# Four pairs' scores in other PSUM banks, products of ones on TensorE in the planned gaps of the first batches, and keys and values pooled by VectorE in one instruction each

## The chip, the cores and the metric

The kernel runs on one NeuronCore of a Trainium2 chip. The metric is the device time of one execution in microseconds (us), lower is better. The core has five engines, each with an instruction queue of its own that is worked off in order: PE (TensorE, matrix products; PEld is its loading of the stationary operand), DVE (VectorE), ACT (ScalarE), POOL (GpSimd) and SP (SyncE, which only issues transfers here). PE writes only to PSUM, which here holds eight tiles ("banks") of 128x512 fp32. Engines wait for each other through semaphores.

## The reference, cut to what matters

Three stages follow one another on 8 batches of 576 rows, 8 heads of 64, model width 512:

```python
def _attn_ref(q, k, v):                       # q, k, v: (8, 8, 576, 64)
    k_p = k.reshape(B, H, 72, 8, D).mean(axis=3)
    v_p = v.reshape(B, H, 72, 8, D).mean(axis=3)
    scores = scale * np.matmul(q, k_p.transpose(0, 1, 3, 2))
    attn = softmax(scores)                    # written out in the original
    return np.matmul(attn, v_p)

def _moe_ref(x, U, V, w_ch1, w_ch2):          # x: (8, 576, 512)
    h = x.transpose(0, 2, 1) @ U @ V
    u = x + h.transpose(0, 2, 1)
    return u + np.maximum(u @ w_ch1, 0.0) @ w_ch2

def _moe2_ref(x, g_ln, w_ch1, w_ch2):         # layer norm, then a second MLP
    xn = (x - mu) / np.sqrt(var + 1e-06) * g_ln
    return x + np.maximum(xn @ w_ch1, 0.0) @ w_ch2
```

Keys and values are averaged over groups of 8 rows ("pooled") before the attention uses them.

## The kernel before

**Two stages.** The first stage (phase_a) takes the attention of one batch after the other, the low-rank step with U and V, and, one group of 512 rows behind it, a first half of the first MLP (8 of its 16 blocks of hidden units, weights resident in SBUF). The second stage (passes) streams the rest of the first MLP and the second MLP through the banks; the change leaves its code alone.

**A pair of heads.** The attention works on 32 pairs of heads, four for each batch. For pair P: load keys, queries and values (att_load); pool the keys and scale them into kbd (att_prep); pool the values into vs (att_prep_v); five products for the scores, 3 of them into one bank and 2 into another (att_s, line 847); a minimum over each row by DVE and ten exponentials by ACT (att_m); ten transposes by PE of the result, copied to SBUF as ef (att_t, transposes at line 398). In the first two batches (P < TM = 8) values follow with the sums of the softmax in an extra column (tm_v, line 1029), DVE divides (tm_n, tiles sm, xg, x), and PE multiplies by U (tm_g, line 1086). At the end of a batch come transposes of xg (tm_t), a copy and a subtraction that make gs (att_gs), products with V (tm_u, line 1120) and the split of the result into two fp32r parts, hid, which is the operand of the MLP (ACT and DVE). The MLP's two layers in the first stage are a_l1 (line 1291, banks "pa", two of them) and a_l2 (line 1319, banks "pbc", two). The other four banks, "py", serve all of the attention. For batch one, tm_g and tm_t also use the MLP's banks, which are idle then.

**Pooling before.** Keys: one TENSOR_REDUCE over 576 elements on DVE, or three adds on POOL, whichever the planner finds sooner done. Values: three adds that halve 512 columns per head to 256, 128 and 64 (lines 818 to 831), each one on DVE or POOL.

**Who sets the order.** A planner (Order.schedule) runs at build time. Every operation has a list of engines with a planned cost, a priority that comes from its place in the program and a bias, and the tiles it uses; the planner steps through planned time and gives each engine its next ready operation. What comes out is a fixed order of instructions for every engine; the chip then works through it in its own time, and only semaphores keep it right. PE's planned cost is doubled while the planner takes TensorE for cold (warm, SLOW).

**Resident weights.** load_w decodes 16 half blocks of 64-bit weights on DVE (four instructions of 128x512, lines 601 to 621), ACT rounds the upper part (wh), and the lower part (wl) is a subtraction, on POOL alone before the change (line 556).

Of the kernel before, what the change touches and what calls it, by code (L numbers as in the profile page):

```python
# [14 lines left out]
ALU = mybir.AluOpType  # L15
AX = mybir.AxisListType
# [6 lines left out]
POOL = 8  # L23
# [78 lines left out]

class Order:
    def __init__(self, nc, tc):
        self.nc, self.tc, self.ops, self.clk, self.bias = nc, tc, [], 0.0, 0.0

    def op(self, engs, fn, r=(), w=(), prio=None, size=0, full=False):
        o = Op()
# [42 lines left out]
    def schedule(self):  # L151
# [61 lines left out]
        while left:  # L213
# [50 lines left out]
                got = other_mode[2]  # L264
            for x in later:
                heapq.heappush(av, x)
            if got is None:
                if later:
                    at(e, t + 150)
                if fut:  # L270
                    at(e, fut[0][0])
                continue
# [93 lines left out]
def c_dve(n):  # L366
    return 68 + 1.042 * n
# [10 lines left out]
def c_pool(n):  # L378
    return 147 + 2.11 * n
# [42 lines left out]
class Kern:  # L422
    def __init__(self, nc, tc, aps):
        self.nc, self.tc = nc, tc
        (self.qT, self.kT, self.v, self.U, self.V, self.wA, self.g, self.wC, self.out) = aps
        self.w_raw = [self.wA, self.wC]
        self.o = Order(nc, tc)
        att = Pool("att")
        stg = Pool("stg")
        slots = Pool("slots", side="right")  # L430
        w = Pool("wres", side="right")
        b1 = Pool("b1", after=[att])
        b2 = Pool("b2", side="right", after=[w])
        ps = Pool("ps", space=PSUM)
        self.pools = [stg, att, slots, w, ps, b1, b2]
        R = self.R = {}

        def ring(pool, name, shape, dt=F32, n=1, fifo=True):
            R[name] = Ring(pool, shape, dt, n, name, fifo)

        ring(stg, "wraw", [128, 512], I64)
        ring(stg, "wx", [128, 512])
        ring(stg, "wt", [128, 512])
        ring(att, "araw", [128, 512], I64)
        ring(att, "ax", [128, 512])
        ring(att, "at", [128, 512])
        ring(att, "kbd", [128, 2, SP], n=2)
        ring(att, "q", [128, S], n=2)
        ring(att, "k", [128, S])
        ring(att, "v", [SP, 2, POOL * D])  # L450
        ring(att, "kp", [128, SP], n=2)
        ring(att, "vs", [SP, 4, D], F32R, 3)
        ring(att, "vz", [SP, 3 * D], n=2)
        ring(att, "ef", [SP, 2, S])
        ring(att, "sc", [128, 5, 2 * SP], n=2)
        ring(att, "mx", [128, 10], n=2)
        ring(att, "sm", [128, 10], n=2)
        ring(att, "eh", [SP, 2, S], F32R)
        ring(att, "el", [SP, 2, S], F32R)
        ring(att, "avt", [128, SH], n=2)  # L460
        ring(att, "xT", [128, S], n=5)
        ring(att, "xh", [128, DM], F32R, 2)
        ring(att, "xl", [128, DM], F32R, 2)
        ring(att, "gr", [128, DM], F32R)
        ring(att, "gs", [128, DM], F32R)
        ring(att, "ust", [128, 5, 128], F32R)
        ring(att, "us", [128, 5, 128])
        ring(att, "vd", [128, S // 4], F32R, 2)
        ring(att, "v1", [SP, 2, D + 1], n=2)
        ring(att, "x4", [128, DM])  # L470
        ring(att, "ut", [128, 4 * 64])
        ring(att, "vstk", [128, S], F32R)
        ring(slots, "op", [128, SLOT], F32R, 16)
        ring(slots, "hid", [128, SLOT], F32R, 8)
        for f in range(NA):
            for a in "hl":
                ring(w, f"w{a}{f}", [128, 1024], F32R)
        ring(w, "xg", [128, NCC, TG])
        ring(w, "ys", [128, TG], n=2)
        for j in range(NSL):  # L480
            pool = b1 if j < NSL - 1 else b2
            for a in "hl":
                ring(pool, f"w1{a}{j}", [128, 7, 256], F32R)
                ring(pool, f"w2{a}{j}", [128, 2, 512], F32R)
        ring(b1, "xraw", [128, NCC, TG])
        ring(b1, "t3", [128, 2, TH])
        ring(b1, "t2", [128, 2, TH])
        ring(b2, "s12", [128, TG], n=2)
        ring(b2, "s5", [128, TH], n=2)
        ring(b2, "res", [128, NCC, TG], n=2)  # L490
        ring(b2, "yt", [128, NCC, TG])
        for a in ("lnh", "lnl"):
            ring(b2, a, [128, TG], F32R)
        for a in ("lns", "lnq"):
            ring(b2, a, [128, TG])
        for a in ("lnv", "lnd"):
            ring(b2, a, [128, TG // 128])
        ring(ps, "pa", [128, 512], n=2)
        ring(ps, "pbc", [128, 512], n=2, fifo=False)
        ring(ps, "py", [128, 512], n=4)  # L500
# [244 lines left out]
    def load_w(self, f, z, way):  # L745

        if z == 0:
            self.wres[f] = self.buf(f"wh{f}"), self.buf(f"wl{f}")
        wh, wl = self.wres[f]
        x = self.decoded(0, f, z, way)  # L750
        c = slice(z * 512, z * 512 + 512)
        self.split(View(wh, z, lambda t: t[:, c]), View(wl, z, lambda t: t[:, c]), View(x, None, lambda t: t), 512, hi_on=(ACT,), lo_on=(GP,))

    def ahead(self, layer, f, z):

# [32 lines left out]
    def att_prep(self, P):  # L788
# [2 lines left out]
        kp, kbd = self.buf("kp"), self.buf("kbd")  # L791
        kv = lambda: k.t.rearrange("p (n s) -> p n s", s=POOL)

        def pool(e):
            if e is nc.vector:
                e.tensor_reduce(kp.t, kv(), axis=AX.X, op=ALU.add)
                return
            for n in (4, 2):
                e.tensor_add(kv()[:, :, :n], kv()[:, :, :n], kv()[:, :, n : 2 * n])
            e.tensor_add(kp.t, kv()[:, :, 0], kv()[:, :, 1])  # L800

        o.op({DVE: c_dve(S), GP: c_pool(4 * SP) + c_pool(2 * SP) + c_pool(SP)}, pool, w=[k, kp])
        for h in range(2):
            r = slice(64 * h, 64 * h + 64)
            o.op(
# [7 lines left out]
    def att_prep_v(self, P):  # L813
# [1 line left out]
        v = self.raw[P][2]  # L815
        vs = self.vs[P] = self.buf("v1" if P < TM else "vz" if P < LEAN_T else "vs")
        n = POOL * D
        while n > D:
            n //= 2
            to, w = (lambda n=n: v.t[:, :, :n]), [v]  # L820
            if P < LEAN_T and n == D:
                to, w = (lambda: vs.t.rearrange("p (a d) -> p a d", d=D)[:, 0:3:2]), [v, vs]
                if P < TM:
                    to = lambda: vs.t[:, :, :D]
            o.op(
                {GP: c_pool(2 * n), DVE: c_dve(2 * n)},
                lambda e, n=n, to=to: e.tensor_add(to(), v.t[:, :, :n], v.t[:, :, n : 2 * n]),
                w=w,
            )
        if P < LEAN_T:  # L830
            return
        self.split(
            View(vs, 0, lambda t: t[:, 0:4:3]),
            View(vs, 1, lambda t: t[:, 1:3]),
            View(v, None, lambda t: t[:, :, :D]),
            2 * D,
        )

    def att_s(self, P, t):
        q, kbd = self.qk[P]  # L840
        if t in (0, 3):
            self.sps[P, t // 3] = self.buf("py")
        ps = self.sps[P, t // 3]
        i = t % 3 * 2 * SP
        self.o.op(
# [498 lines left out]
    def phase_a(self):  # L1344
# [2 lines left out]
        self.xT, self.xhl, self.ut, self.hid, self.wres = {}, {}, {}, {}, {}  # L1347
        self.ud, self.yd, self.wd = {}, {}, {}
        per = self.att_steps()
        self.lean = False  # L1350
        for st in self.biased(per[0], E_BIAS):
            st()
# [476 lines left out]
LAST = ((0, 0), (0, 1), (1, 0), (0, 2), (1, 1), (0, 3), (1, 2), (1, 3))  # L1829
P_BIAS = -20000.0  # L1830
BACC = {"dynamic_dma_scratch_size": 2048}
TM = 2 * NP
E_BIAS = -40000.0
LEAN_T = 8
LEAN_X = 8
W_LEAD = (-12000.0, 8000.0)
# [50 lines left out]
```

## Time and profile before

| what | value |
|---|---|
| runs shown | 1757.46, 1762.2, 1763.09 us, median 1762.2 |
| profiled execution | 1756.11 us, its span 1754.3 us |
| PE busy | 1729.4 us, 99% of the span |
| DVE, ACT, POOL busy | 959.6, 714.5, 753.9 us |

The span runs from the first to the last instruction; the time of the execution has 1.8 us more around it. Busy shares are averages over stages that differ: PE is nearly always busy after the first 100 us, and DVE is busiest in that first part.

### The profile page before, as it was taken

What the parts mean: (1) busy time and instruction counts of PE and PEld (TensorE: products, weight loads), DVE (VectorE), ACT (ScalarE), POOL (GpSimd) and SP (SyncE); (2) the same over time, 40 slices, a digit from 0 to 9 for tenths busy, and PEclk for the clock granted to TensorE, in tenths of its full rate; (3) what the DMA queues carried; (4) which work ended last, traced back from release to release, by engine and by line L of the source; (5) the groups of instructions that cost most, each with busy time, mean ns of one, the idle gap of its engine ahead of it and who ended that gap; (6) DMA issues with size and microseconds to landing.
All of it is one profiled execution on the core that took longest, in us unless ns stands there. A gap on an engine that the chain in (4) does not pass through costs nothing.

```text
span 1754.3 us, 27128 instructions
## 1 busy us (share of the span) xinstructions
PE 1729.4 (99%) x10302; PEld 1525.7 (87%) x10302; DVE 959.6 (55%) x1839; ACT 714.5 (41%) x1812; POOL 753.9 (43%) x655
## 2 busy tenths in 40 slices
PE   6999999999999999999999999999999999999998
PEld 6888888888888899999999889999999999999997
DVE  7998887888655344444445756553225633333333
ACT  5765655655522233333333443333333332223221
POOL 3442312311100166666667643333335455555554
PEclk9999999999999999999999999999999999999999
DMA  6665554555143334444443453431112422333322
GB/s 201 217 201 170 184 182 147 179 174 162 55 165 108 130 111 121 121 121 121 120 121 115 126 163 125 134 121 67 49 49 85 144 103 103 110 119 103 103 79 78
DMA packets 96691, 222.99 MB, mean 127 GB/s; under 512 B 15408, under 2 KB 15792, under 8 KB 90800
## 3 DMA queue, kind: packets, MB, share of 16 engines
q1 hardware_dynamic: 96416, 221.26, 39.9%
q8 instruction: 80, 1.31, 0.3%
q14 instruction: 51, 0.42, 0.1%
q10 hardware_dynamic: 144, 0.00, 0.0%
HBM read 151.85 MB, written 69.37 MB: 126 GB/s over the span
## 4 chain that ended last, share of the span: by engine, by line
PE 91%; DVE 2%; DMA 1%; POOL 0%; issue 0%; ACT 0%; DVEq 0%; POOLq 0%; ACTq 0%
PE py L1608 33%; PE pa L1520 17%; PE pbc L1520 13%; PE pbc L1319 11%; PE pa L1291 11%; PE py L398 2%; PE py L847 2%; PE py L978 1%; PE py L979 1%; PE py L1016 0%; PE py L1015 0%; DVE w1l L556 0%; PE py L1185 0%; PE pbc L1743 0%; DMA wraw<-w_d 0%
## 5 line engine op out<-in xcount | busy, mean ns | idle before, releaser
L1608 PE MATMUL py<-hid,w2h 128*128 128x512 f32 x1728 | 541.2, 394 | 0.2 <-DVE hid L1548 0.2
L1608 PE MATMUL py<-hid,w2l 128*128 128x512 f32 x864 | 338.7, 392 | 0.0
L1520 PE MATMUL pa<-op,w1h 128*128 128x256 f32 x1728 | 326.2, 281 | 1.4 <-DVE s L405 1.0
L1520 PEld LDWEIGHTS pa<-op,w1h 128*128 128x128 f32 x1728 | 293.8, 188 | 37.9 <-DVE s L405 1.5
L556 POOL TENSOR_TENSOR op<-xraw,op 128x512 fp32r<-128x512 f32 x130 | 171.9, 1324 | 276.9 <-ACT op L403 272.0
L1578 DVE TENSOR_TENSOR pbc<-s,pbc 128x512 f32<-128x512 f32 x108 | 75.2, 696 | 382.2 <-PE pbc L1520 382.2
L1608 PEld LDWEIGHTS py<-hid,w2h 128*128 128x128 f32 x1728 | 273.7, 189 | 11.1 <-DVE hid L1548 0.5
L1520 PEld LDWEIGHTS pbc<-op,w1h 128*128 128x128 f32 x1296 | 220.8, 188 | 28.1
L1520 PE MATMUL pbc<-op,w1h 128*128 128x256 f32 x1296 | 244.3, 281 | 0.0
L1520 PE MATMUL pa<-op,w1l 128*128 128x256 f32 x864 | 242.7, 281 | 0.0
L1608 PEld LDWEIGHTS py<-hid,w2l 128*128 128x128 f32 x864 | 162.5, 188 | 36.7
L1319 PE MATMUL pbc<-op,wh 128*128 128x512 f32 x576 | 182.1, 397 | 0.0
L1520 PE MATMUL pbc<-op,w1l 128*128 128x256 f32 x648 | 181.8, 281 | 0.0
L1291 PE MATMUL pa<-hid,wh 128*128 128x512 f32 x576 | 180.5, 394 | 0.0
L1520 PEld LDWEIGHTS pa<-op,w1l 128*128 128x128 f32 x864 | 163.0, 189 | 0.0
L1548 DVE SCALAR_TENSOR_TENSOR hid<-pa,hid 128x512 fp32r<-128x512 f32 x108 | 74.5, 690 | 125.1 <-ACT hid L1542 124.8
L1542 ACT ACTIVATE hid<-pa 128x512 fp32r<-128x512 f32 x108 | 64.6, 598 | 190.8 <-PE pa L1520 180.9
L1542 ACT ACTIVATE hid<-pbc 128x512 fp32r<-128x512 f32 x108 | 64.6, 598 | 180.4 <-DVE pbc L1578 179.5
L1474 POOL TENSOR_TENSOR t<-xraw 128x512 f32<-128x512 f32 x52 | 67.4, 1296 | 141.3 <-DMA xraw<-n_d 89.4
L1291 PEld LDWEIGHTS pa<-hid,wh 128*128 128x128 f32 x576 | 105.8, 188 | 21.3 <-DVE op L1298 0.2
L1520 PEld LDWEIGHTS pbc<-op,w1l 128*128 128x128 f32 x648 | 121.9, 188 | 0.0
L1319 PEld LDWEIGHTS pbc<-op,wh 128*128 128x128 f32 x576 | 103.8, 188 | 19.4
(210 smaller groups left out, 2864.2 us busy)
## 6 DMA issues: line engine op xcount, KB each, us to landing
xraw<-n_d SPq DMA_DIRECT2D x18, 1024.0 KB
wraw<-wC SPq DMA_DIRECT2D x32, 512.0 KB
wraw<-wA SPq DMA_DIRECT2D x24, 512.0 KB
w_d<-wx SPq DMA_DIRECT2D x48, 256.0 KB
wraw<-w_d SPq DMA_DIRECT2D x48, 256.0 KB
k<-kT SPq DMA_DIRECT2D x32, 288.0 KB
q<-qT SPq DMA_DIRECT2D x32, 288.0 KB
v<-v SPq DMA_DIRECT2D x32, 288.0 KB
```

The source lines that it names most:

```text
L398: e.matmul(out, src, ident, start=first, stop=True, is_transpose=True, skip_group_check=True)
L556: lambda e: e.tensor_sub(lo(), src(), hi().bitcast(F32)),
L847: lambda e: e.matmul(ps.t[:, i : i + 2 * SP], q.t[:, QT[t] : QT[t] + 128], kbd.t.rearrange("p h n -> p (h n)"), start=True, stop=True, ski ...
L978: e.matmul(ps.t[:, :SH], w, eh.t[:, h, c], start=True, stop=False)
L1291: e.matmul(ps.t, w.t[:, c], u.t, start=(i == 0), stop=(i == 3 * NCC - 1))
L1319: e.matmul(ps.t, w.t[:, c], x.t, start=(f == 0 and j == 0), stop=(f == NA - 1 and j == 2))
L1474: o.op(on, lambda e: e.tensor_sub(dst(), a(), c()), r=r, w=w)
L1520: e.matmul(bank.t[:, sl], w.t[:, self.WCOL[k], c], u.t[:, t], start=(first and i == 0), stop=(last and i == 5), skip_group_check=True,)
L1542: lambda e: e.activation(h.t[:, :TG], bank.t, AF.Relu),
L1548: lambda e: e.scalar_tensor_tensor(l.t[:, :TG], bank.t, 0.0, h.t[:, :TG].bitcast(F32), op0=ALU.max, op1=ALU.subtract),
L1578: o.op({DVE: c_dve(TG)}, lambda e: e.tensor_add(c.t, s.t, c.t), r=[s], w=[c])
L1608: e.matmul(y.t, w.t[:, i, c], x.t[:, :TG], start=(first and q == 0), stop=(last and q == 2))
```

## The change

It has five parts. The scores of the first four pairs (P < EARLY = 4) go to the MLP's banks pa and no longer to py. Wherever the planner finds nothing for PE between 1.2 and 140 us of planned time, and a bank pbc is free in the plan, it puts a product of the constant tile ones with itself there (128x128x128, planned at 110 ns); its result is never read. Keys are pooled by DVE alone. Values are pooled by DVE in one TENSOR_REDUCE that reads the 8 addends with a stride of 64 elements; for P >= 8 the result goes to a new tile vp. The lower parts wl of the resident weights may go to DVE as well as POOL.

```diff
@@ class Order
+            if got is None and e == PE and self.filler and FILL[0] <= t < FILL[1]:
+                ring, fn = self.filler
+                if ring.free and ring.free[0][0] <= t:
+                    slot = heapq.heappop(ring.free)[1]
+                    free[e], idle = t + FILL[2], 0
+                    warm = min(6000.0, warm + FILL[2])
+                    heapq.heappush(ring.free, (free[e], slot))
...
+                    z.fn = lambda x, slot=slot: fn(x, ring.tiles[slot])
+                    order.append((t, -left, z))
@@ load_w
-        self.split(..., 512, hi_on=(ACT,), lo_on=(GP,))
+        self.split(..., 512, hi_on=(ACT,))
@@ att_prep
-        def pool(e):
...
-        o.op({DVE: c_dve(S), GP: c_pool(4 * SP) + c_pool(2 * SP) + c_pool(SP)}, pool, w=[k, kp])
+        o.op({DVE: c_dve(S)}, lambda e: e.tensor_reduce(kp.t, kv(), axis=AX.X, op=ALU.add), w=[k, kp])
@@ att_prep_v
-        while n > D:
-            n //= 2
...
-                {GP: c_pool(2 * n), DVE: c_dve(2 * n)},
-                lambda e, n=n, to=to: e.tensor_add(to(), v.t[:, :, :n], v.t[:, :, n : 2 * n]),
+        def pool(e):
+            e.tensor_reduce(to(), v.t.rearrange("p h (s d) -> p h d s", s=POOL), axis=AX.X, op=ALU.add)
+
+        o.op({DVE: c_dve(2 * n)}, pool, w=[v, vp])
@@ att_s
-            self.sps[P, t // 3] = self.buf("py")
+            self.sps[P, t // 3] = self.buf("pa" if P < EARLY else "py")
@@ phase_a
+        self.o.filler = self.R["pbc"], lambda e, ps: e.matmul(
+            ps[:, :128], self.ones, self.ones, start=True, stop=True, skip_group_check=True
+        )
@@ constants
+EARLY = 4
+FILL = (1200.0, 140000.0, 110.0)
```

The planner makes a new order from this. PE's queue at the very start of the program, before the change (254 to 257 are the banks py; ident marks a transpose, ef a product with the values):

```order
L847 MATMUL py_254<-kbd_154,q_156 128x144 x3
L847 MATMUL py_255<-kbd_154,q_156 128x144 x2
L847 MATMUL py_256<-kbd_155,q_157 128x144 x2
L398 MATMUL py_257<-ident,sc_168 72x128 x4
L847 MATMUL py_256<-kbd_155,q_157 128x144
L847 MATMUL py_254<-kbd_155,q_157 128x144
L398 MATMUL py_255<-ident,sc_168 72x128 x4
L847 MATMUL py_254<-kbd_155,q_157 128x144
L398 MATMUL py_257<-ident,sc_168 72x64 x2
L1029 MATMUL py_255<-v_193,ef_167 128x65 x6
```

The same place of the changed kernel (251 and 252 are the banks pa, 253 and 254 pbc; where the dots stand, the two rows of ones alternate until there are 28):

```order
L848 MATMUL pa_251<-kbd_154,q_156 128x144 x3
L848 MATMUL pa_252<-kbd_154,q_156 128x144 x2
L1351 MATMUL pbc_253<-ones 128x128
L1351 MATMUL pbc_254<-ones 128x128
...
L411 MATMUL py_255<-ident,sc_169 72x128 x4
L411 MATMUL py_256<-ident,sc_169 72x128 x4
L848 MATMUL pa_251<-kbd_155,q_157 128x144 x3
L848 MATMUL pa_252<-kbd_155,q_157 128x144 x2
L411 MATMUL py_257<-ident,sc_169 72x64 x2
L1030 MATMUL py_258<-v_194,ef_168 128x65 x6
```

The second pair's scores stood between the first pair's scores and its transposes; now they stand behind the transposes, and 28 products of ones stand in their place. In all the changed order has 92 products of ones on PE, all of them ahead of the MLP's first product; the other 64 stand in blocks of 1 to 10, between the pairs of batch one and around the products with V at its end.

DVE's queue between the gs of batch one and the split of the products with V, before the change:

```order
L1171 SCALAR_TENSOR_TENSOR gs_188<-gr_187,neg_b,pbc_252 128x512
L1050 TENSOR_SCALAR sm_172<-py_254 128x6
L1050 TENSOR_SCALAR sm_172<-py_257 128x4
L827 TENSOR_TENSOR v_159<-v_159 72x2x256
L1057 RECIPROCAL sm_172<-sm_172 128x6
L827 TENSOR_TENSOR v_159<-v_159 72x2x128
L1057 RECIPROCAL sm_172<-sm_172 128x4
L827 TENSOR_TENSOR v_193<-v_159 72x2x64
L1067 TENSOR_TENSOR x_195<-py_257,sm_172 128x128
L872 TENSOR_REDUCE mx_170<-py_256 128x6
L556 TENSOR_TENSOR hid_218<-pa_250,hid_217 128x512
```

And of the changed kernel, from the same instruction on:

```order
L1172 SCALAR_TENSOR_TENSOR gs_189<-gr_188,neg_b,pbc_253 128x512
L615 TENSOR_SCALAR at_153<-at_153 128x512
L1051 TENSOR_SCALAR sm_173<-py_255 128x6
L620 TENSOR_SCALAR at_153<-at_153 128x512
L1058 RECIPROCAL sm_173<-sm_173 128x6
L570 TENSOR_TENSOR wl_234<-wx_146,wh_233 128x512
L828 TENSOR_REDUCE v_194<-v_159 72x2x64
L1051 TENSOR_SCALAR sm_173<-py_258 128x4
L808 TENSOR_REDUCE kp_161<-k_158 128x72
L570 TENSOR_TENSOR hid_219<-pa_251,hid_218 128x512
```

Three adds have become one reduction, a pooling of keys and a lower part of the weights have come over from POOL's queue, and two steps of a decode now stand ahead of the first hid.

PE's queue behind that place, in the changed kernel, from the first product with V to the last product of ones:

```order
L1121 MATMUL pa_251<-vstk_198,gs_189 128x512
L1121 MATMUL pa_252<-vstk_198,gs_189 128x512
L1148 MATMUL pbc_254<-vstk_198,gs_189 128x64 x4
L848 MATMUL py_257<-kbd_154,q_156 128x144 x2
L1351 MATMUL pbc_253<-ones 128x128 x8
L411 MATMUL pa_251<-ident,xg_245 128x128 x4
L1121 MATMUL pa_251<-vstk_198,gs_189 128x512
L1351 MATMUL pbc_253<-ones 128x128
L411 MATMUL pa_252<-ident,xg_245 128x128 x4
L1121 MATMUL pa_252<-vstk_198,gs_189 128x512
L1351 MATMUL pbc_254<-ones 128x128
...
```

Before the change the same products stood there without the rows of ones, and the MLP's first product came one pair earlier in the queue: ahead of it stood 35 score products, 80 transposes and 50 products with values, now 38, 84 and 60.

## Rows read from the trace of the kernel before

**Rows 1.** Windows: us; busy us (instructions) of PE, PEld, DVE, ACT, POOL; granted clock.
```profile
0.00:20.00 20.00, 10.85 (x46) 9.83 (x47) 12.72 (x39) 9.95 (x31) 5.32 (x24) 1.00 0.74 215
20.00:40.00 20.00, 16.97 (x120) 14.92 (x119) 15.44 (x39) 9.94 (x33) 9.51 (x11) 1.00 0.68 206
40.00:60.00 20.00, 16.33 (x128) 14.46 (x128) 18.96 (x47) 16.28 (x49) 8.10 (x10) 1.00 0.65 207
60.00:80.00 20.00, 19.47 (x121) 16.47 (x120) 18.91 (x46) 12.40 (x34) 6.46 (x5) 1.00 0.67 222
80.00:100.00 20.00, 18.55 (x121) 16.39 (x120) 19.81 (x42) 10.87 (x37) 11.17 (x12) 1.00 0.55 166
100.00:120.00 20.00, 20.00 (x106) 16.43 (x106) 17.52 (x36) 14.09 (x43) 6.63 (x5) 1.00 0.72 234
```

**Rows 2.** PE in order of time: start, us, passes, idle time before and its releaser.
```profile
5.35 2.74 PE L847 MATMUL py<-kbd,q 128*128 128x144 f32 x10 [5.35 <-DMA q<-qT]
11.89 1.30 PE L847 MATMUL py<-kbd,q 128*128 128x144 f32 x4 [3.80 <-issue]
12.98 1.06 PE L398 MATMUL py<-ident,sc 128*72 128x128 f32 x4
13.83 1.17 PE L847 MATMUL py<-kbd,q 128*128 128x144 f32 x4
...
16.62 4.53 PE L1029 MATMUL py<-v,ef 72*128 72x65 f32 x20
...
28.07 2.34 PE L1029 MATMUL py<-v,ef 72*128 72x65 f32 x20
...
38.59 0.71 PE L847 MATMUL py<-kbd,q 128*128 128x144 f32 x4
39.13 0.60 PE L398 MATMUL py<-ident,sc 128*72 128x128 f32 x4
```

**Rows 3.** PE in order of time, at the end of batch one and where layer two begins.
```profile
58.25 0.66 PE L398 MATMUL pa<-ident,xg 128*128 128x128 f32 x4 [1.37 <-DVE hid L556]
...
61.83 0.73 PE L1291 MATMUL pa<-hid,wh 128*128 128x512 f32 x2
...
105.75 0.62 PE L1319 MATMUL pbc<-op,wh 128*128 128x512 f32 x2
```

**Rows 4.** DVE by line and shape, first 110 us: count, busy us, mean ns of one.
```profile
L827 DVE TENSOR_TENSOR v<-v 72x512 f32<-72x512 f32 x11 | 9.2, 840 | 2.4 <-DMA v<-v 2.4
...
L613 DVE SCALAR_TENSOR_TENSOR ax<-araw,at 128x512 int32<-128x512 int32 x7 | 6.3, 902 | 0.4
L872 DVE TENSOR_REDUCE mx<-py 128x6 f32<-128x432 f32 x10 | 6.0, 598 | 3.1 <-PE py L847 3.1
...
L796 DVE TENSOR_REDUCE kp<-k 128x72 f32<-128x576 f32 x7 | 5.2, 742 | 3.6 <-DMA k<-kT 3.6
L827 DVE TENSOR_TENSOR v<-v 72x256 f32<-72x256 f32 x7 | 5.0, 720 | 0.1
...
L872 DVE TENSOR_REDUCE mx<-py 128x4 f32<-128x288 f32 x9 | 4.0, 450 | 1.5 <-PE py L847 1.5
...
L827 DVE TENSOR_TENSOR v<-v 72x128 f32<-72x128 f32 x8 | 3.5, 441 | 0.0
```

**Rows 5.** DVE in order of time: two instructions of one shape, then gs of batch two.
```profile
27.71 0.68 DVE L613 SCALAR_TENSOR_TENSOR ax<-araw,at 128x512 int32<-128x512 int32 x1
...
30.00 1.65 DVE L613 SCALAR_TENSOR_TENSOR wx<-wraw,wt 128x512 int32<-128x512 int32 x1
...
96.51 0.73 DVE L1171 SCALAR_TENSOR_TENSOR gs<-gr,neg_b,py 128x512 fp32r<-128x512 f32 x1
```

**Rows 6.** POOL in order of time: beside the second of them, and two pooling steps.
```profile
29.84 1.27 POOL L556 TENSOR_TENSOR wl<-ax,wh 128x512 fp32r<-128x512 f32 x1 [6.86 <-ACT wh L403]
...
41.02 0.31 POOL L800 TENSOR_TENSOR kp<-k 128x72 f32<-128x72 f32 x1
41.29 0.45 POOL L827 TENSOR_TENSOR v<-v 72x128 f32<-72x128 f32 x1
```

More of the change, by code (lines that the diff above doesn't have):

```diff
@@ L104, in __init__ @@
     def __init__(self, nc, tc):
-        self.nc, self.tc, self.ops, self.clk, self.bias = nc, tc, [], 0.0, 0.0
+        self.nc, self.tc, self.ops, self.clk, self.bias, self.filler = nc, tc, [], 0.0, 0.0, None
     def op(self, engs, fn, r=(), w=(), prio=None, size=0, full=False):
@@ L266, in schedule @@
                 heapq.heappush(av, x)
+            if got is None and e == PE and self.filler and FILL[0] <= t < FILL[1]:
[5 more added lines that the diff above has]
+                    heapq.heappush(ring.free, (free[e], slot))
+                    z = Op()
+                    z.eng, z.start, z.end, z.bufs = PE, t, free[e], ()
+                    z.fn = lambda x, slot=slot: fn(x, ring.tiles[slot])
+                    order.append((t, -left, z))
+                    at(e, free[e])
+                    continue
             if got is None:
@@ L452, in __init__ @@
         ring(att, "vs", [SP, 4, D], F32R, 3)
+        ring(att, "vp", [SP, 2, D])
         ring(att, "vz", [SP, 3 * D], n=2)
@@ L751, in load_w @@
         c = slice(z * 512, z * 512 + 512)
-        self.split(View(wh, z, lambda t: t[:, c]), View(wl, z, lambda t: t[:, c]), View(x, None, lambda t: t), 512, hi_on=(ACT,), lo_on=(GP,))
+        self.split(View(wh, z, lambda t: t[:, c]), View(wl, z, lambda t: t[:, c]), View(x, None, lambda t: t), 512, hi_on=(ACT,))
     def ahead(self, layer, f, z):
@@ L792, in att_prep @@
         kv = lambda: k.t.rearrange("p (n s) -> p n s", s=POOL)
-        def pool(e):
[L795 to L800, printed above, removed]
-        o.op({DVE: c_dve(S), GP: c_pool(4 * SP) + c_pool(2 * SP) + c_pool(SP)}, pool, w=[k, kp])
+        o.op({DVE: c_dve(S)}, lambda e: e.tensor_reduce(kp.t, kv(), axis=AX.X, op=ALU.add), w=[k, kp])
         for h in range(2):
@@ L817, in att_prep_v @@
         n = POOL * D
-        while n > D:
-            n //= 2
[L820 to L825, printed above, removed]
-                {GP: c_pool(2 * n), DVE: c_dve(2 * n)},
-                lambda e, n=n, to=to: e.tensor_add(to(), v.t[:, :, :n], v.t[:, :, n : 2 * n]),
-                w=w,
-            )
-        if P < LEAN_T:
+        vp = vs if P < TM else self.buf("vp")
+        to = (lambda: vp.t[:, :, :D]) if P < TM else (lambda: vp.t)
+        def pool(e):
+            e.tensor_reduce(to(), v.t.rearrange("p h (s d) -> p h d s", s=POOL), axis=AX.X, op=ALU.add)
+        o.op({DVE: c_dve(2 * n)}, pool, w=[v, vp])
+        if P < TM:
             return
@@ L834, in att_prep_v @@
             View(vs, 1, lambda t: t[:, 1:3]),
-            View(v, None, lambda t: t[:, :, :D]),
+            View(vp, None, lambda t: t),
             2 * D,
```

## The prediction

> **What bounds the kernel now.** I read the windows of the first 120 us first, because the page's 99% for PE leaves so little idle time that the reader must see where it lies. PE is busy 82.17 us of the first 100 [rows 1], so 17.83 us are idle there; over the whole span 25 us are (1754.3 less 1729.4), and from 100 us on PE is full. Whatever the change gives must come from the start, or be lost by a new wait later.
>
> Then PE's order of time. It waits 5.35 us for the first load and 3.80 us between the first and the second pair's scores [rows 2]; the other 8.7 us (17.83 - 5.35 - 3.80) are some dozen short waits, the longest named one 1.37 us for DVE's split of a product with V [rows 3]. The reader should also see that equal work is not equally long: twenty passes of a values product take 4.53 us at 16.6 us and 2.34 us at 28 us; a pass of the scores takes 0.274 us at 5.35 us (2.74 / 10) and 0.135 us at 38.6 us (four from 38.59 to 39.13) [rows 2]. The granted clock is given as 1.00 in every window [rows 1], but these durations are those of 1.2 GHz and 2.4 GHz: the clock rose somewhere in the 20s, although PE had worked with few gaps since 11.89.
>
> Last, DVE: 19 to 19.8 of 20 us busy between 40 and 100 us [rows 1], so in that stretch it is nearly as much the bound as PE. Both must be counted.
>
> **PE's account up to layer two of the MLP**, the first instruction of which starts at 105.75 [rows 3]. Up to there both orders hold the same real work, so the account can be compared.
>
> Before: 105.75 - 17.83 idle = 87.9 us of work. Of this, 30 passes of scores (three pairs) cost 0.139 us too much each, 4.2 us; the first values 2.2 us (4.53 - 2.34); twelve transposes 0.115 us each (four take 1.06 us against 0.60), 1.4 us [rows 2]. So 7.8 us are the low clock, and 80.1 us is the work at full speed.
>
> After: 5.35 us for the load, which nothing touches; 80.1 us of work; the first pair's scores still at the low level, 10 x 0.139 = 1.4 us. Products of ones are in no trace. The nearest row is a transpose, also 128x128: 0.21 us at the low level (12.98 to 13.83 for four [rows 2]), so half of that, 0.106 us, at the high one. 92 of them at 0.106 us are 9.8 us. How many run at the low level is the unknown: at least none, at most all 28 of the first block and more. I take half the block, 14, because the block makes PE busy without a gap from 5.35 us on, which the old start never was: 14 x 0.106 = 1.5 us more. Sum: 98.1 us.
>
> To this come waits that the products don't cover. They replace idle time (3.80 + 8.7 = 12.5 us before, 9.8 us of products now), but they stand in a fixed order, and a wait that is longer than its block remains. Lower bound none, upper bound 8.7 us, if the short waits all stay. I take 2 us, near the row that I expect to stay: the 1.37 us wait for hid [rows 3]. In the new DVE queue a 128x512 subtraction, a value and a key pooling and two decode steps stand ahead of that first hid; behind it on PE wait the transposes into the two pa banks, then the remaining products with V. So layer two starts at about 100.1 us, 5.6 us earlier than 105.75.
>
> **Banks.** Scores of pairs 0 to 3 in pa free two of the four py banks for transposes and values. What it saves is part of the short waits counted above; it costs nothing, since pa is used by nobody before the first batch's transposes. A product of ones writes a pbc bank, so it can wait for a reader of it (gs, or the copy of the last 64 columns of U's product, which stands behind the same DVE queue); that is in the 2 us.
>
> **DVE's account**, to the gs of batch two, which ends the stretch (96.51 us before [rows 5]) and which PE's last products with V need. Values: adds of 9.2 + 5.0 + 3.5 = 17.7 us are on DVE in 110 us, the rest on POOL [rows 4]. Now there are eleven reductions up to gs. A reduction of 432 elements takes 598 ns and one of 288 takes 450 ns [rows 4], 1.03 ns for an element, so 1024 elements take 598 + 592 x 1.03 = 1208 ns, if the stride of 64 elements is free: 13.3 us, 4.4 us less. Keys: eleven instead of seven at 0.742 us [rows 4], 3.0 us more. Five lower parts of weights, a subtraction of 512 columns like the decode step of 0.68 us [rows 5]: 3.4 us more. Together 2.0 us more. Against it: DVE is held when POOL works. The step of 0.68 us takes 1.65 us when it starts 0.16 us behind a POOL instruction of 1.27 us [rows 5, 6]; its mean in the stretch is 0.90 us [rows 4]. With most pooling gone from POOL, that 0.2 us comes off some 15 such steps, 3 us. DVE's load is thus unchanged within 1 us, and to be 5.6 us earlier it must give up idle time: it has 20 - 12.72 and 20 - 15.44 idle in the first 40 us, 11.8 us in all [rows 1], mostly waits for scores and loads. Earlier scores shorten these. I take it that it follows.
>
> **The stride.** POOL's last step of the keys reads every eighth element, 72 of them, in 0.31 us; its step of 128 adjacent elements takes 0.45 us [rows 6], the same time for an element or less: no price for a stride of 8 is seen, on the other engine. No DVE row reads with such a stride. The bounds are 1.21 us (free) and twice the streaming part, 2.26 us; I take the free end because of POOL's row. The Trainium skill, page SBUF — State Buffer, says in the box on cachelines that accesses which each go to a new 16-byte line pay a penalty, and four fp32 is how far one can go for free. By that, every element here would pay; the sum would be that of rival A.
>
> **After layer two has begun** PE is full, and the second stage is as before. DVE has 2.5 of 20 us to spare at 100 to 120 us [rows 1]; four reductions of a batch replace adds of about the same length, so I count nothing there. PE's full queue of MLP products hides it; if that cover goes, it costs what rival A says of the later batches.
>
> **Sum.** 1756.1 - 5.6 = 1750.5 us on the scale of the profiled execution. The runs shown lie above it: the four times known (1756.1, 1757.5, 1762.2, 1763.1) have a mean 3.6 us above the profiled one, the median 6.1 us. If part of that spread is the moment at which the clock rises, steady products take it away. I put the time at 1752 us, between 1750.5 and 1750.5 + 3.6. Its own range: no waits and an early rise give 1747, 5 us of waits and the full spread 1757.
>
> **Rivals.**
>
> A, the stride costs double: 11 x 1.05 = 11.6 us more on DVE up to gs. About 4 us are hidden in the idle start, the rest, 7.6 us, eats the 5.6 us: layer two starts 2 us late, 1758. Then every batch has 4.2 us more of DVE in some 64 us of which DVE had an eighth free, and lower parts and keys on top: 1 us of waits for each of six batches or more, 1764, up to 1770. For: the page, and DVE's nearly full stretch. Against: POOL's row. It decides from about 1.7 us for a reduction (0.5 us x 11 = 5.6 us), and from 2 us it is slower than before.
>
> B, the products do not raise the clock before the twenties, or hold PE longer than the waits. Then the first 47, which stand ahead of the third pair's transposes, take 0.21 us, 9.9 us, where the waits were 3.80 us and about 1 us: 5 us lost, against some 4 us for the second pair's order and banks and for the short waits later. 1758 on the same scale, 1768 if the low level lasts to the fourth pair. For: PE worked from 11.89 to the twenties without a rise. Against: it had real gaps before, and none from 5.35 on now.
>
> C, DVE does not give up its idle time: gs stays where it is, less 1 us. PE runs through its products and waits at gs. The gain is 1 us, 1756.
>
> **Chances.** Likeliest 0.58, A 0.17, B 0.10, C 0.15. The range 1745 to 1763 holds the likeliest, C and the lower half of A and B; below it 0.04, above it 0.14. About 0.3% (5.3 us) is what a measurement of this kernel can tell from no change; against the median 1762.2 that is faster below 1756.9 and slower above 1767.5. Faster: 0.55 of the likeliest and 0.05 of C, 0.60. Slower: 0.09 of A, 0.05 of B, 0.01 of C, 0.15. Same: 0.25.
>
> **What will show it.** Right: values products of the first pair at 0.117 us a pass; granted clock or durations at 2.4 GHz from about 10 to 12 us; layer two from 99 to 101 us; reductions of values at about 1.2 us; PE full behind that. Wrong: reductions at 2 us or more (A); scores of the second pair at 0.27 us a pass (B); PE waiting for DVE's gs or xg between 60 and 100 us (C), or new waits for DVE beyond 110 us, which I have counted at nothing.

## The result, and the profile after

The change made the kernel slower: 1775.26 us (median of 6 runs, 1769.64 to 1775.9) against 1762.64 us (6 runs, 1757.46 to 1767.42), a ratio of 1.006 with the interval [1.0041, 1.0079] (the medians alone give 1.0072; the ratios in this document are those on record with their 95% intervals). The forecast was 1752 us. The profiled execution took 1770.87 us, its span 1769.0 us.

Windows of the changed kernel, same columns as [rows 1] (behind the granted clock stand the busy share of the DMA engines and GB/s), with longer windows at the end:

```profile
0.00:20.00 20.00, 14.84 (x111) 14.12 (x112) 14.33 (x35) 10.74 (x36) 2.79 (x20) 1.00 0.77 222
20.00:40.00 20.00, 19.25 (x165) 18.31 (x164) 18.21 (x44) 10.86 (x40) 2.54 (x2) 1.00 0.73 211
40.00:60.00 20.00, 19.67 (x157) 18.09 (x156) 19.86 (x44) 14.79 (x43) 1.28 (x1) 1.00 0.62 207
60.00:80.00 20.00, 20.00 (x134) 17.82 (x133) 19.83 (x42) 13.61 (x48) 1.30 (x1) 1.00 0.59 185
80.00:100.00 20.00, 19.33 (x111) 16.31 (x110) 19.98 (x39) 10.86 (x21) 2.59 (x2) 1.00 0.54 170
100.00:120.00 20.00, 15.92 (x77) 12.24 (x77) 17.82 (x37) 16.11 (x57) 4.18 (x3) 0.91 0.76 256
120.00:140.00 20.00, 17.96 (x79) 14.58 (x78) 16.83 (x29) 8.84 (x33) 0.86 (x1) 0.91 0.47 148
140.00:160.00 20.00, 19.71 (x108) 16.58 (x107) 18.72 (x38) 14.04 (x52) 0.46 (x1) 1.00 0.57 172
160.00:200.00 40.00, 39.47 (x210) 32.34 (x209) 34.79 (x70) 21.52 (x74) 5.22 (x5) 1.00 0.56 185
200.00:300.00 100.00, 97.95 (x519) 81.25 (x518) 89.41 (x173) 58.49 (x207) 9.89 (x10) 1.00 0.54 166
300.00:500.00 200.00, 196.65 (x1029) 162.72 (x1028) 160.06 (x334) 111.59 (x387) 19.85 (x18) 1.00 0.40 134
```

The start is what was hoped for: PE is idle 6.9 us in the first 100 us instead of 17.8. But PE, full from 100 us on before, now has 4.1 and 2.0 us idle between 100 and 140 us, both windows at a granted clock of 0.91 in the mean, 0.8 us between 140 and 200 us, and 5.4 us between 200 and 500 us. The first product of the second stage starts at 612.2 us, where it started at 598.3 us before: nearly the whole loss lies in the first stage.

PE in order of time, against [rows 2, 3]:

```profile
5.04 2.74 PE L848 MATMUL pa<-kbd,q 128*128 128x144 f32 x10 [5.04 <-DMA q<-qT]
7.40 3.74 PE L1351 MATMUL pbc<-ones 128*128 128x128 f32 x28
...
12.14 1.46 PE L848 MATMUL pa<-kbd,q 128*128 128x144 f32 x10
...
13.76 2.45 PE L1030 MATMUL py<-v,ef 72*128 72x65 f32 x20
...
97.08 0.62 PE L1320 MATMUL pbc<-op,wh 128*128 128x512 f32 x2
```

The second pair's scores run at the high level already (0.146 us a pass), and layer two begins at 97.08 us, 8.7 us earlier than before and 3 us earlier than forecast.

DVE by line and shape over the whole span (count, busy us, mean ns), against [rows 4]:

```profile
L828 DVE TENSOR_REDUCE vp<-v 72x128 f32<-72x1024 f32 x24 | 47.3, 1972 | 0.3
...
L828 DVE TENSOR_REDUCE v<-v 72x128 f32<-72x1024 f32 x8 | 15.5, 1936 | 3.0 <-DMA v<-v 2.7 <-PE py L1030 0.2
```

A reduction of the values takes 1.94 to 1.97 us where the sum took 1.21.

The longest waits of PE between 140 and 500 us of the changed kernel (us in total, times, longest):

```profile
PE py L848 <- DVE xT L987: 2.0, 3, 0.7
PE py L1186 <- DVE gs L1172: 1.5, 4, 0.5
```

The shorter ones behind them are waits for DVE too. A wait at 129 us, ahead of these, shows how a slow reduction reaches PE. In order of time, DVE, ACT and PE:

```profile
128.35 1.91 DVE L828 TENSOR_REDUCE vp<-v 72x128 f32<-72x1024 f32 x1
...
130.29 0.30 ACT L416 CAST vs<-vp 72x128 fp32r<-72x128 f32 x1 [3.76 <-DVE vp L828]
130.50 0.58 ACT L416 COPY ys<-pbc 128x512 f32<-128x512 f32 x1
...
131.13 1.22 PE L1320 MATMUL pbc<-op,wh 128*128 128x512 f32 x2 [2.04 <-ACT ys L416]
132.14 0.63 PE L1320 MATMUL pbc<-op,wl 128*128 128x512 f32 x1
```

The reduction holds ACT's cast of vs; queued behind that cast is the copy ys, which empties the bank that PE's next product needs. PE stands for 2.04 us, and the first products behind it run at the low level (0.63 us for one of wl, against 0.39 at 128.7 us, ahead of the wait). The stride is only a part of this wait: with adjacent addends (first experiment below) PE still stands 1.37 us at the same place.

### The profile page after: what moved, and what is told of

Same layout as the page of the kernel before. It is cut to its first block, busy times and chain, and to the rows that moved or that the text cites. A ratio compares the mean times of both kernels' runs of the same rounds, so it can differ in the third digit from the quotient of the medians.

```text
span 1769.0 us, 27175 instructions
## 1 busy us (share of the span) xinstructions
PE 1742.3 (98%) x10394; PEld 1532.3 (87%) x10394; DVE 989.3 (56%) x1842; ACT 720.1 (41%) x1824; POOL 666.9 (38%) x542
## 4 chain that ended last, share of the span: by engine, by line
PE 77%; DVE 10%; DMA 3%; issue 2%; ACT 1%; POOL 0%; SPq 0%; DVEq 0%; ACTq 0%; POOLq 0%
PE py L1612 33%; PE pa L1524 17%; PE pbc L1524 12%; PE pbc L1320 7%; PE pa L1292 4%; DVE vp L828 2%; PE py L411 1%; DVE xT L987 1%; DMA wraw<-wC 1%; DVE el L570 1%; DMA wraw<-wA 1%; DVE wx L627 1%; PE py L848 1%; DVE wx L635 1%; DVE op L1299 1%
## 5 line engine op out<-in xcount | busy, mean ns | idle before, releaser
L1524 PEld LDWEIGHTS pa<-op,w1h 128*128 128x128 f32 x1728 | 293.7, 188 | 38.7 <-DVE s L418 2.2
L1292 PEld LDWEIGHTS pa<-hid,wh 128*128 128x128 f32 x576 | 105.7, 188 | 21.4 <-DVE op L1299 0.4
```

The source lines that it names most:

```text
L1292: e.matmul(ps.t, w.t[:, c], u.t, start=(i == 0), stop=(i == 3 * NCC - 1))
L1524: e.matmul(bank.t[:, sl], w.t[:, self.WCOL[k], c], u.t[:, t], start=(first and i == 0), stop=(last and i == 5), skip_group_check=True,)
```

## The experiments

Times are medians; each ratio is to the kernel before, timed beside it on the same chip. Two variants were not always timed side by side, so differences between them are given by the medians and by the ratios.

### The reduction with adjacent addends

The queues of all engines stay as in the changed kernel; only the access pattern differs.

```diff
-v.t.rearrange("p h (s d) -> p h d s", s=POOL)
+v.t.rearrange("p h (d s) -> p h d s", s=POOL)
```

> The changed kernel in its exact order, but each value reduction adds eight adjacent elements instead of eight that lie 64 elements apart (same count, same tiles, so the pooled values are not the reference's). Theory stride: a reduction takes 1.2 us instead of 1.95, VectorE is no longer late behind 97 us, layer two still starts at 97 us, PE loses less than 3 us between 97 and 500 us, and the time is 1748 to 1755 us, faster than before by about 0.5%. Rival load: the instructions that came over from GpSimd are too many whatever the stride; the reduction gets shorter but PE still loses 8 us or more behind 97 us, time above 1762. Rival order: the waits come from the new order of PE and not from VectorE; time stays at 1770 or above.

Measured: 1760.29 us, ratio 0.9987 [0.9973, 1.0002]. DVE by line and shape:

```profile
L828 DVE TENSOR_REDUCE vp<-v 72x128 f32<-72x1024 f32 x24 | 29.0, 1209 | 0.3
...
L828 DVE TENSOR_REDUCE v<-v 72x128 f32<-72x1024 f32 x8 | 9.7, 1217 | 6.1 <-DMA v<-v 5.5 <-PE py L1030 0.4
```

The same instruction on as many elements takes 1.21 us. The stride costs 0.75 us of each reduction, 24 us of DVE in all (62.8 against 38.7), and 13 us (by the ratios) to 15 us (by the medians) of the kernel's time. But the time misses the 1748 to 1755 us that I expected: the start's gain does not reappear, although layer two begins at 98.2 us here, and the kernel can't be told from the one before.

That layer two is 1.1 us later here than in the changed kernel, with less work on DVE, is within what the clock cost. In this execution it fell once more on the way:

```profile
45.00:57.00 12.00, 11.99 (x102) 11.14 (x100) 11.23 (x28) 9.76 (x29) 0.00 (x0) 1.00 0.76 238
57.00:60.40 3.40, 3.40 (x16) 3.16 (x16) 1.95 (x4) 1.20 (x2) 1.26 (x1) 0.50 0.63 202
```

3.4 us at half the clock are 1.7 us of work lost, which the changed kernel did not lose there.

### Three adds on DVE in place of the reduction

```diff
-e.tensor_reduce(to(), v.t.rearrange("p h (s d) -> p h d s", s=POOL), axis=AX.X, op=ALU.add)
+for m in (n // 2, n // 4):
+    e.tensor_add(v.t[:, :, :m], v.t[:, :, :m], v.t[:, :, m : 2 * m])
+e.tensor_add(to(), v.t[:, :, :D], v.t[:, :, D : 2 * D])
```

> The changed kernel in its exact order, but each value pooling is three adds of halves on VectorE (512, 256 and 128 columns), issued one behind the other at the same place, with the same planned cost. Theory stride: the three adds take 0.60 + 0.34 + 0.20 us to the next issue, 1.15 us, so this gives the same time as the adjacent reduction, 1748 to 1755 us. Rival load: above 1762 us. If adjacent reductions recover the time and this does not, the saving of instructions counts, not the stride.

Measured: 1765.55 us, ratio 1.0011 [1.0001, 1.0022]. The adds take 0.68, 0.45 and 0.29 us, 1.42 us together: dearer than 1.21, cheaper than 1.97, and the time lies between, 10 us above what I expected. Layer two starts at 102.05 us in the profiled execution, 3.8 us later than with adjacent addends; the clock rose later there (last section). This is the changed kernel with its worst cost mended, and it is still not faster than before.

### Without the products of ones

```diff
-        self.o.filler = self.R["pbc"], lambda e, ps: e.matmul(
-            ps[:, :128], self.ones, self.ones, start=True, stop=True, skip_group_check=True
-        )
```

> The changed kernel without the products of ones (planned again; the strided reductions stay). Theory: the products gave the early rise of the clock, about 6 us of the 8.7 us by which layer two came earlier; without them layer two starts at 102 to 105 us, the later loss for VectorE stays, and the time is 1774 to 1782 us. Rival: since VectorE is the bound from 97 us on, an earlier start only makes PE wait longer, and the time without them is within 3 us of the changed kernel's. Second rival: the products hold PE and cost time; the time is under 1768 us.

Measured: 1780.66 us, ratio 1.0105 [1.0085, 1.0125]: 5.4 us slower than with them by the medians, 7.9 us by the ratios. Layer two starts at 110.11 us, later than the 102 to 105 us expected and later than before the change. The granted clock is 0.86, 0.83 and 0.83 in the windows from 20 to 80 us, where it is 1.00 with the products. PE in order of time shows one of the falls:

```profile
24.21 1.11 PE L1087 MATMUL pbc<-xg,us 128*128 128x128 f32 x8
...
32.03 0.86 PE L411 MATMUL pa<-ident,xg 128*128 128x128 f32 x4 [1.68 <-ACT sc L882]
32.69 1.91 PE L1087 MATMUL pbc<-xg,us 128*128 128x128 f32 x8
```

Eight products with U take 1.11 us, and 1.91 us behind an idle time of 1.68 us. So the products are worth something beside strided reductions. The planner made another order without them, and no run separates that from the products themselves.

### The planner told what the reduction costs

```diff
-        o.op({DVE: c_dve(2 * n)}, pool, w=[v, vp])
+        o.op({DVE: 1860}, pool, w=[v, vp])
```

> The changed kernel with the planned cost of a value reduction set to what the trace shows to the next issue, 1.86 us, instead of 1.135 us; the planner makes another order from it. Theory: most of the loss is VectorE's load and not the planner's ignorance of it, so at most a third of the 23 us lost behind 97 us comes back, time 1764 to 1773 us. Rival: with the cost known the planner puts the late work elsewhere and nearly all comes back, time 1750 to 1758 us.

Measured: 1772.69 us, ratio 1.0058 [1.0038, 1.0078]. The order that the planner makes with the true cost does not rescue it.

### The parts alone, on the kernel before

The start alone (banks and products, old pooling, lower parts on POOL), the pooling alone (with the lower parts free, no banks, no products), the banks alone:

```diff
 # start alone, banks alone
-            self.sps[P, t // 3] = self.buf("py")
+            self.sps[P, t // 3] = self.buf("pa" if P < EARLY else "py")
 # start alone
+        self.o.filler = self.R["pbc"], lambda e, ps: e.matmul(
 # pooling alone
-        o.op({DVE: c_dve(S), GP: c_pool(4 * SP) + c_pool(2 * SP) + c_pool(SP)}, pool, w=[k, kp])
+        o.op({DVE: c_dve(S)}, lambda e: e.tensor_reduce(kp.t, kv(), axis=AX.X, op=ALU.add), w=[k, kp])
...
+            e.tensor_reduce(to(), v.t.rearrange("p h (s d) -> p h d s", s=POOL), axis=AX.X, op=ALU.add)
```

> The kernel before with the banks for four pairs and the products of ones, but with the old pooling and the old lower parts (adds and lower parts may go to GpSimd). Theory load: since the adjacent reduction alone only came back to the time of before, VectorE has taken on too much from GpSimd; with its old load the early start is kept, layer two starts at 98 to 103 us, PE loses under 2 us between there and 500 us, time 1752 to 1757 us. Rival: VectorE was already the second bound in the stretch from 40 to 100 us, so an earlier PE gains nothing in any pooling; time 1759 to 1764 us.

> The kernel before with the pooling and the lower parts of the change alone: strided reductions on VectorE, no products, scores in their old banks. Theory stride and load: VectorE is late from the start, as in the changed kernel, and there is no early start to set against it; time 1775 to 1783 us. Rival: what costs is the early start together with the load (PE waits and its clock falls); alone the pooling costs under 8 us, time below 1770 us.

> The kernel before with the scores of the first four pairs in the MLP's banks, and nothing else. Theory: the short waits for banks are 1 to 2 us of the start and the clock's rise stays in the twenties; time 1759 to 1763 us, no change that can be told. Rival: the banks and the order that they allow are what brought layer two forward by 8.7 us; time 1752 to 1757 us.

Measured: start alone 1766.2 us, ratio 1.0012 [0.9998, 1.0026]; pooling alone 1774.27 us, 1.0061 [1.0041, 1.0081]; banks alone 1763.52 us, 1.0001 [0.9992, 1.0011]. The pooling alone is as slow as the whole change. There layer two starts at 112.46 us, in an execution whose granted clock was 0.88 in the mean of the first 100 us. The other two bring layer two to 99 us, and gain nothing; the start alone, at 1766.2 us, lies above what both theories gave it. Windows of 100 to 140 us, start alone and then banks alone:

```profile
100.00:120.00 20.00, 12.76 (x66) 9.38 (x64) 18.51 (x35) 17.04 (x62) 12.53 (x13) 0.88 0.74 238
120.00:140.00 20.00, 19.98 (x86) 16.57 (x87) 14.63 (x33) 9.82 (x38) 4.61 (x3) 0.86 0.38 112
```

```profile
100.00:120.00 20.00, 15.92 (x86) 13.12 (x84) 19.37 (x36) 15.62 (x55) 9.09 (x10) 0.91 0.79 255
120.00:140.00 20.00, 19.59 (x89) 16.18 (x90) 16.87 (x37) 10.75 (x43) 5.01 (x6) 0.91 0.45 150
```

PE stands for 7.2 us and 4.1 us between 100 and 120 us, where it stood for none before [rows 1], and the granted clock falls. The strided reductions are in neither of these two, so they can't be the cause.

### Three adds, lower parts on GpSimd again

```diff
-hi_on=(ACT,))
+hi_on=(ACT,), lo_on=(GP,))
```

> The changed kernel with three adds on VectorE for the values, and the lower parts of the weights back on GpSimd alone. Theory load: ten subtractions of 0.6 us less on VectorE in the first 115 us, but more time held behind GpSimd; against the run with three adds alone 2 to 5 us come back, time 1760 to 1763 us. Rival: the lower parts were moved at a place where VectorE had room; time 1765 us as with three adds alone.

Measured: 1764.98 us, ratio 1.0013 [0.9999, 1.0027]: it can't be told from three adds alone (1.0011). Where the lower parts are made made no difference that these runs show.

### DVE relieved of part of the decode

With the start's gain gone at 100 to 140 us in every variant, I asked whether DVE's load takes it. In three kernels the last step of 18 decodes was cut to 16 columns, in unchanged order.

```diff
+        def low_bits(e):
+            self.cut = getattr(self, "cut", 0) + 1
+            c = slice(0, 16 if self.cut <= 18 else n)
+            e.scalar_tensor_tensor(xu()[:, c], part(0).bitcast(U32)[:, c], 29, xu()[:, c], ...
```

> The changed kernel with the same order, but the last step of the first 18 decodes (the step that puts the lowest bits into a weight or input) does 16 columns instead of 512; the lowest three bits are left out there, and nothing else. Each of these steps should take some 0.06 us instead of 0.68 us, so VectorE is relieved of 18 x 0.62 = 11 us in the first 130 us, some 7 us of it between 60 and 120 us. Theory D (after the early start VectorE is the bound up to the third batch): layer two starts earlier than 97 us, TensorE's idle time and low clock between 100 and 140 us shrink from 6.1 us to 2 us or less, and the time falls by 5 to 8 us to 1763 to 1768 us, the strided reductions of the later batches still costing what they cost. Theory L (a chain of scores, ScalarE and VectorE latencies in TensorE's fixed order sets the wait at 100 to 140 us): the reductions of idle time are under 2 us and the time stays at 1770 to 1775 us.

> The version with adjacent reductions (it adds eight adjacent elements, so pooled values are not the reference's) and the same relief of 18 decodes, whose lowest three bits are left out. Theory D: layer two starts at about 95 us or earlier, TensorE is full between 100 and 140 us but for 1 to 2 us (5.5 us idle without the relief), group two starts at 198 to 200 us instead of 203.7, and the time is 1753 to 1756 us, ratio to the kernel before about 0.995 to 0.997. Theory L: idle time at 100 to 140 us stays at 4 to 6 us and the time at 1759 to 1761 us.

> The kernel before with the same relief of 18 decodes, whose lowest three bits are left out: the control. TensorE is full there from 100 us on, so only the idle time ahead of layer two can shrink. If VectorE already sets that start, layer two starts 3 to 5 us earlier than 105.7 and the time falls as much, to 1757 to 1760 us (theory D would give it here too). If its waits are those of scores and loads, layer two starts within 2 us of 105.7 and the time stays within 2 us of the kernel before.

Measured: changed kernel 1772.68 us, ratio 1.0062 [1.0046, 1.0078]; adjacent 1757.01 us, 0.998 [0.9968, 0.9991]; before 1759.45 us, 0.9989 [0.9976, 1.0003]. A cut step takes 0.165 us, not the 0.06 expected, so the relief is 18 x 0.52 = 9.3 us. By the medians it brings 2.6, 3.3 and 3.0 us, by the ratios none, 1.2 and 1.9 us; no one of these is clear of its intervals. Layer two does not move (96.9, 98.1 and 105.7 us, against 97.1, 98.2 and 105.7). Only the first pair is a clean comparison: the clock rose within the block of 28 in both. In the relieved adjacent version it rose behind the block (6.24 us for it, against 4.27), and in the relieved kernel before it fell again (granted clock 0.76 between 20 and 40 us, 1.00 without the relief); what the relief gave there may have gone into that. The idle time between 100 and 140 us goes from 6.1 to 4.5 and from 5.5 to 3.7 us. So this relief takes away a quarter to a third of that idle time; a larger one follows.

### Four steps of the decode cut

The version with adjacent reductions once more, now with sign, clamp, shift and low bits cut, for decodes 7 to 24:

```diff
+        def few(step):
+            k = self.cuts = getattr(self, "cuts", {})
+            k[step] = k.get(step, 0) + 1
+            return slice(0, 16 if 6 < k[step] <= 24 else n)
```

> The version with adjacent reductions, in the same order, with four of the five steps of 18 decodes (those that begin between about 45 and 140 us) cut from 512 to 16 columns: sign, clamp, shift and low bits; the decoded weights are not the reference's there. VectorE is relieved of about 18 x 1.3 = 23 us and ScalarE of some 6 us. Theory L (the third batch's attention is held by its own chain: scores, exponentials on ScalarE, values, copy, add, and four banks that come free one after the other, while the fixed order has no MLP products left to fill in): layer two still starts at 97 to 99 us, TensorE still loses 2.5 to 4 us between 100 and 140 us (3.7 with the low bits alone cut, 5.5 with none), and the time is 1755 to 1757 us. Theory D2 (it is the decode's steps on VectorE and ScalarE, which stand between the chain's steps in their queues): idle time between 100 and 140 us falls to 1.5 us or less, the clock does not fall there, and the time is 1751 to 1754 us.

Measured: 1756.53 us, ratio 0.9971 [0.9956, 0.9987]. Windows of 100 to 140 us, with adjacent reductions alone and with the four steps cut:

```profile
100.00:120.00 20.00, 15.87 (x84) 12.64 (x84) 18.00 (x37) 15.82 (x56) 3.52 (x3) 0.91 0.77 257
120.00:140.00 20.00, 18.63 (x93) 15.33 (x93) 16.96 (x32) 10.83 (x38) 1.52 (x1) 1.00 0.48 148
```

```profile
100.00:120.00 20.00, 17.14 (x86) 13.54 (x85) 17.02 (x41) 15.97 (x66) 3.59 (x3) 0.91 0.75 239
120.00:140.00 20.00, 20.00 (x101) 16.72 (x100) 15.43 (x37) 10.45 (x39) 0.00 (x0) 1.00 0.61 193
```

2.9 us of the 5.5 remain, and the clock still falls. In order of time, PE, ACT and DVE of the kernel with the four steps cut:

```profile
107.71 0.40 PE L984 MATMUL py<-eh,vs 72*128 72x288 f32 x1 [0.60 <-ACT sc L887]
110.09 0.76 PE L853 MATMUL py<-kbd,q 128*128 128x144 f32 x4 [1.85 <-DVE xT L992]
...
107.79 0.81 ACT L416 COPY avt<-py 64x288 f32<-64x288 f32 x2
...
108.42 0.90 DVE L907 TENSOR_TENSOR sc<-sc,sm 128x720 f32<-128x720 f32 x1
109.24 0.43 DVE L620 TENSOR_SCALAR at<-at 128x16 f32<-128x16 f32 x1
109.59 0.93 DVE L992 TENSOR_TENSOR xT<-py,avt 64x288 f32<-64x288 f32 x2
```

And the same place of the changed kernel, PE and DVE:

```profile
110.03 0.77 PE L848 MATMUL py<-kbd,q 128*128 128x144 f32 x4 [1.83 <-DVE xT L987]
...
109.20 0.42 DVE L615 TENSOR_SCALAR at<-at 128x512 f32<-128x512 f32 x1
```

PE has multiplied with the values of one pair of the third batch into its last bank; its next row in the queue is the scores of a later pair, which need a bank of py. The bank comes free when ACT has copied half of it (avt), DVE has normalised the next pair's scores (0.90 us, ahead in DVE's queue) and has added the halves (xT). One step of a decode (at) stands in DVE's queue between these two. It was cut to 16 columns here, yet it took 0.43 us, as long as with 512 in the changed kernel, although the same step on the tile wt, cut alike, takes 0.165 us in the mean. So the cut took nothing out of this wait, and that the wait is the same here (1.85), in the changed kernel and with adjacent reductions (1.83 each) does not show it to be free of the decode; 0.35 us of it (109.24 to 109.59) are the decode's. The rest are steps of the attention itself. Theory L has its numbers (2.9 us idle, 1756.53 us) and D2 has not, but D2 is not wholly wrong: 2.6 of the 5.5 us went with the decode, the later wait for ys between 120 and 140 us among them.

## Why the prediction was wrong

**The stride, the step that failed.** "I take the free end because of POOL's row" [rows 6] put the value reduction at 1.21 us; it takes 1.94 to 1.97 us, near the other bound of 2.26. POOL's row, a step of 72 elements on another engine, says nothing of DVE. Nor does it read as the prediction has it: 0.31 us for 72 elements are 4.3 ns each, 0.45 us for 128 are 3.5 ns, so "the same time for an element or less" holds only if a fixed part of each step is taken off first, which was not worked out. The adjacent version, in which only the access pattern differs, shows the stride to be the cause (1.21 us, and 1760.29 us for the kernel), and the pooling alone is as slow as the whole change. Rival A had the mechanism; its range (1764, up to 1770) lies a little low, and its threshold (1.7 us) was not tried, since no variant measured a reduction between 1.42 and 1.94 us. The Trainium skill, page SBUF — State Buffer, box on cachelines, says that accesses which each go to a new line pay; these rows agree, 1.97 against 1.21 us.

**Where it costs.** Rival A expected 2 us at layer two and the rest behind it. In the changed kernel layer two was not late: 11 reductions took 8 us more on DVE, yet gs of batch two came at 91.50 us instead of 96.51 [rows 5]. The loss came later, by waits for DVE in the batches that followed, for which the sum said "I count nothing there". With adjacent reductions no wait of PE is shown between 140 and 500 us, and the second stage starts at 599.7 us; with the stride, 200 to 500 us alone hold 5.4 us of idle time, and it starts at 612.2 us.

**PE's account up to layer two was right, by its terms a little high.** 97.1 us against 100.1. The waits left are 1.9 us (6.9 idle less 5.04 for the load; taken: 2), but that is luck: the wait for hid, which was expected to stay, shrank to 0.3 us, and waits of 0.7 us each for gs and for x (the divided values) took its place. The block of 28 took 3.74 us, 0.77 more than 28 x 0.106, so about 7 products ran at the low level (taken: 14). The work at full speed comes out as 97.1 - 5.04 - 1.9 - 1.4 - 9.8 - 0.8 = 78.2 us instead of 80.1.

**The second failed step: that the gain of the start is kept.** The sum subtracted it from the whole time. Rival C had the size (1756, "DVE does not give up its idle time") but not the place: gs did come earlier. PE arrives earlier at the third batch's attention and waits there. It also has another order there: in the changed kernel four products with values stand in a row, at 105.6 to 107.9 us, and the scores behind them, while before the change products of the MLP stood between them:

```profile
115.92 0.29 PE L978 MATMUL py<-eh,vs 72*128 72x288 f32 x1
...
116.18 0.63 PE L1319 MATMUL pbc<-op,wh 128*128 128x512 f32 x2
...
118.95 0.30 PE L978 MATMUL py<-eh,vs 72*128 72x288 f32 x1
```

Every variant with the early start has a new order as well, so no run separates the early arrival from the order. With adjacent reductions this can be added up: layer two 105.75 - 98.2 = 7.5 us earlier; then 4.1 + 1.4 us idle between 100 and 140 us, and 0.09 x 20 = 1.8 us of clock, 7.3 us. The ratio, 0.9987, can't be told from no gain. For the wait of 1.8 us the rows show what holds PE: 0.90 us of normalising, 0.35 us of a decode step and the addition, one behind the other on DVE. Of the 5.5 us, 2.6 went with the decode's steps; the rest is the attention's chain and DVE's and ACT's queues together.

**DVE's account.** That DVE "follows" at the start was right, and in the changed kernel its load was not what set layer two: 9.3 us less on DVE moved it by 0.2 us. In the other two kernels layer two stood still as well, but the clock went otherwise there.

**The clock.** That steady products make the rise come early was right for the profiled execution, and not reliably so (below). The price that rival B feared was not seen in the time: the start alone, with products, and the banks alone, without, do not differ beyond their intervals.

**What stays open.** Of the 14.8 us between the two profiled executions, the rows name 8.7 gained, 12.1 us more of idle time from 100 to 500 us, and twice 1.8 us of clock, 7.0 us in sum. The rest is in PE's time booked as busy, between 100 and 500 us most of all, where fewer products stand in the same time (519 from 200 to 300 us and 1029 from 300 to 500 us, before the change 530 and 1059); the ends of matmuls are modelled, so waits that are short would be hidden there. No run here separates them. No version was clearly faster than before while computing the same.

## What to carry to other kernels

Price a strided reduction from a row of the same engine with the same stride, or measure that instruction by itself, before the rest of the sum is made; a row of another engine is no bound. A gain in a start-up stretch counts only as far as the next stage can take it: look for the stage's own chain (here banks that come free one after the other) and for the ready work that would cover its waits if the engine came there earlier. An engine that is nearly full need not be the bound: take some of its work away and see whether the milestone moves, and check first that the clock did the same in both executions.

## What the runs showed of the hardware that I had not expected

With one order on PE, the block of 28 products after the first scores took 3.74 us (changed kernel), 4.27 (adjacent), 4.06 and 3.98 (relieved), and 6.24 us in two others. One of these, with three adds on DVE, PE in order of time:

```profile
5.18 2.74 PE L850 MATMUL pa<-kbd,q 128*128 128x144 f32 x10 [5.18 <-DMA q<-qT]
7.54 6.24 PE L1353 MATMUL pbc<-ones 128*128 128x128 f32 x28
...
15.28 2.54 PE L850 MATMUL pa<-kbd,q 128*128 128x144 f32 x10
17.98 2.45 PE L1032 MATMUL py<-v,ef 72*128 72x65 f32 x20
```

Here all 28 and most of the next ten scores ran at 1.2 GHz (0.22 and 0.25 us a pass), and only the values at 2.4 GHz; in the changed kernel the rise came within the block. The moment of the rise thus differs by 6 us or more between executions in which PE had done the same.

In the trace of before, PE stays at the high level once it is there, as far as its first 500 us go; with the same order on PE and the decode relieved, it fell again between 20 and 40 us (granted clock 0.76). In every variant with the early start the level falls between 110 and 119 us, in or right behind a wait of 1.8 to 4.4 us: 1.83 us in the changed kernel and 4.44 us with the start alone, where the granted clock is 0.88 and 0.86 in the windows of 100 to 120 and 120 to 140 us.

A fall came without a wait, too. With adjacent reductions PE was busy for 11.99 of the 12 us before 57.0 us, with scores, transposes, products of ones, with V and with values, and the granted clock from 57.0 to 60.4 us was 0.50 (the rows stand in the first experiment). The changed kernel, with the same order on PE, had no fall there.
